# Gated linear attention into a gated state-space block: the second group's output product by seven half-block products, and where the weight sums lie

## The chip, the cores and the metric

The kernel runs on one core of a Trainium2 chip. The metric is the device time of one execution in microseconds, the median of several runs. Engine names follow the profile: PE (TensorE matmul), PEld (its weight loads), DVE (VectorE), ACT (ScalarE), POOL (GpSimd), SP (SyncE, which here only issues DMAs).

## The reference, cut to what matters

Batch 4, 8 heads, 768 steps, head size 48, model size 384, inner size 512, all in fp32:

```python
for t in range(S):                       # attention, per batch and head
    state = alpha[t][:, None] * state + outer(k[t], v[t])
    y[t] = q[t] @ state
x = y, heads side by side                # (4, 768, 384)
val, gate = split(x @ w_in)              # 2 x 512 columns
h[t] = exp(A_log) * h[t-1] + val[t]
f = silu(gate) * h
out = f @ w_out                          # (4, 768, 512) @ (512, 384)
```

The last line is what the change is about. `w_in` and `w_out` arrive as 64-bit floats and are turned to fp32 on the chip.

## The kernel before, in words

The 4 x 768 steps are cut into 12 groups of 256 steps (`n` = 0 to 11, three to a batch). A Python loop over `n` writes the whole order out by hand (`manual_schedule`), so each engine's queue is in program order, and an instruction waits only by semaphores for what it reads or overwrites. In the turn of group n, TensorE does the projections of group n (`project`, L988, four chunks `cc` of the inner size, 128 channels each), the attention of group m = n + 1 (`scores` L798, `values` L834, `states` L866, `carried` L847), and an output. DVE does, for a group two or so ahead, the transposes of alpha, k and q (L600), the running products P (`scan_P`, L635) and their inverses V (`scan_V`, L654), the scaled keys Zk (L619) and queries Zq (L610). For group n it does the state scan `hh` of each chunk (L995). The product f = silu(gate) x hh (L1008) is made on DVE for groups 0, 1 and 11 and on POOL for the others. Below, f0 to f3 and hh0 to hh3 are those of chunks 0 to 3.

The output f @ w_out of a group is done in one of two ways:

- `output` (L1011), groups 0 and 1: eight matmuls of 128x384 into two PSUM banks, two evictions on ACT (L1016), two DMAs from SP (L1017).
- `output_parts` (L1067), groups 2 to 10: the product is seen as a 2x2 by 2x2 block product and done with seven half-block products (L1064) in place of eight, each of two matmuls of 128x192. This needs sums of the weights, T1 to T4 (`sum_weights`, L1040 to L1044, on POOL, once), and sums of f, S1 to S4 (S3 at L1055 and S1 at L1058 on POOL, S2 and S4 at L1059 and L1060 on DVE). ACT copies three products out of PSUM (`s1`, `s7`, `s5`) and evicts a quarter; DVE adds the rest (U2 at L1092, then L1093 and L1094), POOL one quarter (L1090, L1095); SP sends the two rows blocks (L1097).

The seven products run on TensorE in the order written: pa with B11, pd with S3 and T3, then pc with S1 and T1, pa with B21 (it adds to the first one's bank), pd with T4, pb with S2 and T2, pc with S4 and B22. The profile counts every fp32 matmul twice, so a product of two matmuls stands as x4 and one whole output as x28.

`T1` to `T3` lie in `wide`, which in turn 0 and until the end of `output(0)` holds f of group 0. So `sum_weights` waits for that output's last matmul. f of groups 1 to 11 all lie in the one buffer `f_last`.

PSUM banks for projections, scores and outputs are four (`mm0` to `mm3`), and the string `taken` says by hand which one each request takes. A matmul into a bank waits until the bank's last reader is done. Three row buffers `o_sb` hold results on their way out.

In turn 1 (`n == 1`, L1229 to L1268) the part touched is, in order of writing: third(2) (its last DMAs are issued by POOL and SP at L963), f1, the scan V, project chunk 2, Zk, f2, `output(0)`, `sum_weights`, project chunk 3, transpose of q (L1264), its reload, Zq (L1266), f3, and the transposes of alpha and k for group 4; after it `output(1)` (L1348), and `first(3)`'s scores at the head of turn 2.

Of the kernel before, what the change touches and what calls it, by code (L numbers as in the profile page):

```python
# [9 lines left out]
FP32 = mybir.dt.float32  # L10
# [336 lines left out]
def fast(  # L347
# [22 lines left out]
    nc = tc.nc  # L370
    B, H, S, D = q.shape
    DM = H * D
    DI = moe_A_log.shape[0]
    C = 128
    G = 2
# [231 lines left out]
    def scaled_q(m, t, P, c=None):  # L607
        u0, n = (0, 2 * G) if c is None else (2 * c, 2)
        at = ds(u0 * L, n * L)
        nc.vector.tensor_mul(Zqs[m % 2][:, ds(u0, n), :, D:].rearrange("p u h t -> p h u t"),  # L610
                             t[:, :, at].rearrange("p h (u t) -> p h u t", t=L),
                             P[:, :, 1:GP][:, :, at].rearrange("p h (u t) -> p h u t", t=L))
# [48 lines left out]
    def products(m):  # L661
# [17 lines left out]

    taken = iter("0321032103231023" "1023102310231023" "102310231023" "10"
                 "23012301" "230132" "01230123" "012310" "23012301" "230132" "01230123" "012310"
                 "23012301" "230132" "01230123" "012310" "23012301" "230132" "01230123" "012310"
                 "23012301" "0132" "01320132")

    def bank(tag=None):
        if tag:
            return ps_at.tile([C, 512], FP32, tag=tag, name=tag)
        return ps_mm.tile([C, 512], FP32, tag=f"mm{next(taken)}", name="mm")  # L690
# [255 lines left out]
    for h in range(H):  # L946
        i, e, s = h // 4, h % 4 // 2, h % 2 ^ h // 4
        at = D * h
# [79 lines left out]
    HM = DM // 2  # L1028
    KC = NI // 2
    blocks = [[w_outs[k][:, :, ds(HM * i, HM)] for i in range(2)] for k in range(KC)]  # L1030
    flat = wide.rearrange("p c x -> p (c x)")
    sums_w = [flat[:, ds(KC * HM * i, KC * HM)].rearrange("p (a n) -> p a n", a=KC) for i in range(3)]
    T4 = [wide_S[i][:, 0:HM] for i in range(KC)]
    s1, s7 = flat[:, ds(3 * KC * HM, HM)], wide_S[2][:, 0:HM]
    parts_f = {}

    def sum_weights():
# [13 lines left out]
    def quarter(row, col):  # L1051
        return f_last[:, ds(KC * col, KC), ds(C * row, C)]
# [1 line left out]
    def sum_early():  # L1054
        nc.gpsimd.tensor_sub(parts_f["S3"], quarter(1, 0), quarter(0, 0))  # L1055

    def sum_late():
        nc.gpsimd.tensor_add(parts_f["S1"], quarter(1, 0), quarter(1, 1))  # L1058
        nc.vector.tensor_add(parts_f["S2"], quarter(1, 1), parts_f["S3"])  # L1059
        nc.vector.tensor_sub(parts_f["S4"], quarter(0, 1), parts_f["S2"])  # L1060

    def product(o, a, b, start):
        for k in range(KC):
            nc.tensor.matmul(o, a[:, k], b[k] if type(b) is list else b[:, k], start=start and k == 0,  # L1064
                             stop=k == KC - 1, skip_group_check=True)

    def output_parts(n):  # L1067
        b, g = divmod(n, NG)
        (B11, B12), (B21, B22) = blocks
        T1, T2, T3 = sums_w  # L1070
        S1, S2, S3, S4, U2, s5 = (parts_f[x] for x in ("S1", "S2", "S3", "S4", "U2", "s5"))
        copy = lambda to, t: nc.scalar.activation(to, t, AF.Copy)
        pa, pd = [bank()[:, 0:HM] for _ in range(2)]
        product(pa, quarter(0, 0), B11, True)
        copy(s1, pa)
        product(pd, S3, T3, True)
        yield
        copy(s7, pd)
        yield
        pc = bank()[:, 0:HM]  # L1080
        product(pc, S1, T1, True)
        copy(s5, pc)
        product(pa, quarter(0, 1), B21, False)
        o_sb = [rows.tile([C, DM], FP32, tag="o_sb", name="o_sb") for _ in range(G)]
        copy(o_sb[0][:, 0:HM], pa)
        product(pd, quarter(1, 1), T4, False)
        pb = bank()[:, 0:HM]
        product(pb, S2, T2, True)
        product(pc, S4, B22, False)
        nc.gpsimd.tensor_add(s7, s7, s5)  # L1090
        yield
        nc.vector.tensor_add(U2, s1, pb)  # L1092
        nc.vector.tensor_add(o_sb[1][:, 0:HM], U2, pd)  # L1093
        nc.vector.tensor_add(o_sb[0][:, HM:], U2, pc)  # L1094
        nc.gpsimd.tensor_add(o_sb[1][:, HM:], U2, s7)  # L1095
        for c in range(G):
            nc.sync.dma_start(out=out[b, ds(g * GC + c * C, C), :], in_=o_sb[c])  # L1097
        yield
# [16 lines left out]
    def go(count):  # L1115
        for _ in range(count):
            next(steps, None)
# [73 lines left out]
    for n in range(N):  # L1191
# [37 lines left out]
        elif n == 1:  # L1229
# [22 lines left out]
            load_raw("k", 4, nc.sync)  # L1252
            load_v(4, nc.sync)
            f1()
            junk(3)
            V = scan_V(3, P)
            f2 = project(n, 2)
            scaled_k(3, tk, V)
            f2()
            output(0)  # L1260
            sum_weights()
            f3 = project(n, 3)
            tq = plain("q")
            turn("q", tq)  # L1264
            load_raw("q", 4, nc.sync)
            scaled_q(3, tq, P)  # L1266
            f3()
            go(2)  # L1268
        else:
            if n == 2:  # L1270
                first(m)
# [72 lines left out]
            load_v(m + 2, nc.sync)  # L1344
        if n == N - 2:
            check_flag()
        if n == 1:
            output(n)  # L1348
        if n == N - 2:
            for _ in outs:  # L1350
                pass
# [5 lines left out]
@with_exitstack  # L1357
def kernel(ctx: ExitStack, tc: tile.TileContext, *args):
    nc = tc.nc
    out = args[-1]  # L1360
    C, GC, NI = 128, 256, 4
    B, S, DM = out.shape
    keep = ctx.enter_context(tc.tile_pool(name="keep", bufs=1))
    ps_mm = ctx.enter_context(tc.tile_pool(name="ps_mm", bufs=1, space=bass.MemoryType.PSUM))
    w_outs = [keep.tile([C, 2, DM], FP32, name=f"w_out{i}") for i in range(2)]
    f_last = keep.tile([C, NI, GC], FP32, name="f_last")
    rows = ctx.enter_context(tc.tile_pool(name="rows", bufs=3))
    with tc.manual_schedule():
        good = fast(tc, *args, w_outs, f_last, ps_mm, rows)
    with tc.If(good <= 0, preferred_fallthrough_block=True, label="last") as choice:  # L1370
        general(tc, *args, w_outs)
    with choice.Else(), tc.manual_schedule():
        half = DM // 2
        for i, c, at, size in ((0, 0, 0, DM), (1, 1, 0, half), (3, 1, half, half)):
# [41 lines left out]
```

## Time and profile before

| what | us |
|---|---|
| median of 3 runs (lowest, highest) | 269.58 (269.56, 270.09) |
| the profiled execution, its own time | 270.68 |
| its span in the trace | 269.0 |
| TensorE busy | 263.0 |
| VectorE busy | 233.5 |
| GpSimd busy | 165.3 |

The trace is of the profiled execution; the 1.68 us beside its span are start and end, which no engine shows. It ran 1.1 us longer than the median run. In the rows, a start is counted from the start of the span, and a duration is that of one instruction or, where "x" is above 1, of a merged run of them. The last part of a row in brackets is idle time ahead of it and who ended it.

### The profile page before, as it was taken

To read this page: it belongs to the slowest core of one execution; us is meant where nothing else is said; L and a number is where in the kernel's file an instruction comes from. 1 tells how busy PE (TensorE), PEld (TensorE's weight loads), DVE (VectorE), ACT (ScalarE), POOL (GpSimd) and SP (SyncE) were. 2 spreads that over 40 slices of the span, in tenths; PEclk is the share of its full clock that TensorE was granted. 3 is DMA by queue.
4 is the path that set the end of the run, shared out by engine and by line. 5 is a ranking of instruction groups with operands and counts; after the bars stand their busy time and mean duration, and the time that the engine had idled before them with its cause. 6 is when DMAs were issued, how large, how long until landed. Compare 5 with 4: busy or idle time off the path is not lost.

```text
span 269.0 us, 9976 instructions
## 1 busy us (share of the span) xinstructions
PE 263.0 (98%) x4168; PEld 230.2 (86%) x4168; DVE 233.5 (87%) x316; ACT 111.6 (41%) x270; POOL 165.3 (61%) x185
## 2 busy tenths in 40 slices
PE   7989999999999999999999999999999999999995
PEld 5978889886688988988988988988988989988974
DVE  7978898996999999999999999999999998883440
ACT  4666776281242631632543533524524515314011
POOL 8222304093267998996985995996886987646000
PEclk9999999999999999999999999999999999999999
DMA  5938974796993659559687478569588501201201
GB/s 173 316 117 281 296 172 139 210 225 159 243 220 90 138 159 231 119 140 229 133 227 170 107 207 184 113 173 219 128 210 172 144 3 29 75 3 37 70 7 59
DMA packets 52304, 41.19 MB, mean 153 GB/s; under 512 B 27392, under 2 KB 50944, under 8 KB 52256
## 3 DMA queue, kind: packets, MB, share of 16 engines
q1 hardware_dynamic: 49328, 37.34, 56.1%
q0 software_dynamic: 1536, 2.20, 3.1%
q10 hardware_dynamic: 1392, 0.99, 1.3%
q8 instruction: 34, 0.56, 0.9%
q14 instruction: 14, 0.11, 0.1%
HBM read 32.54 MB, written 4.72 MB: 139 GB/s over the span
## 4 chain that ended last, share of the span: by engine, by line
PE 96%; DMA 2%; issue 0%; ACTq 0%; ACT 0%
PE mm L988 48%; PE mm L1064 16%; PE y L834 4%; PE y L847 4%; PE mm L1022 4%; PE s L798 4%; PE mm L798 3%; PE s L866 3%; PE mm L707 2%; PE mm L1377 2%; DMA raw_q<-in_q_dram 2%; PE mm L702 2%; PE mm L703 1%; PE y L918 1%; PE mm L750 1%; PE y L926 1%
## 5 line engine op out<-in xcount | busy, mean ns | idle before, releaser
L988 PE MATMUL mm<-xT,w_in 128*128 128x256 f32 x576 | 129.4, 382 | 0.0
L988 PEld LDWEIGHTS mm<-xT,w_in 128*128 128x128 f32 x576 | 107.9, 190 | 16.0 <-issue 0.5
L1006 ACT ACTIVATE sg<-mm 128x256 f32<-128x256 f32 x48 | 18.4, 383 | 88.9 <-PE mm L988 88.9
L1008 POOL TENSOR_TENSOR f_last<-sg,hh 128x256 f32<-128x256 f32 x36 | 28.8, 806 | 26.1 <-ACT sg L1006 22.6
L886 POOL TENSOR_TENSOR sum<-sum,dS 128x192 f32<-128x192 f32 x30 | 39.3, 1310 | 3.0 <-ACT dS L874 1.4
L635 DVE TENSOR_TENSOR_SCAN P<-al,lower 128x1028 f32<-128x1028 f32 x12 | 30.5, 2541 | 0.3
L995 DVE TENSOR_TENSOR_SCAN hh<-a_dec,hh,mm 128x256 f32<-128x256 f32 x32 | 23.3, 728 | 8.4 <-PE mm L988 8.2
L654 DVE TENSOR_TENSOR_SCAN V<-al,ends 128x1028 f32<-128x1028 f32 x12 | 28.5, 2375 | 0.4
L963 POOL DMA_DIRECT2D xT<-yst x44 | 22.6, 518 | 5.4 <-ACT yst L960 4.0
L556 POOL TENSOR_TENSOR w_in<-w_in,wr 128x768 int32<-128x768 int32 x4 | 7.3, 1820 | 26.3 <-DVE wbits L1143 9.3
L1064 PE MATMUL mm<-wide,wr 128*128 128x192 f32 x108 | 20.8, 327 | 0.0
L600 DVE STREAM_TRANSPOSE k<-raw_k 128x1024 f32<-128x1024 f32 x9 | 18.5, 2053 | 0.0
L600 DVE STREAM_TRANSPOSE q<-raw_q 128x1024 f32<-128x1024 f32 x9 | 18.2, 2026 | 0.0
L1064 PEld LDWEIGHTS mm<-wide,wr 128*128 128x128 f32 x108 | 18.0, 190 | 0.0
L874 ACT ACTIVATE dS<-s 128x384 f32<-128x384 f32 (+1 forms) x18 | 7.4, 461 | 24.4 <-PE s L866 24.4
L818 POOL TENSOR_TENSOR AK<-AK,mask 128x512 f32<-128x512 f32 x9 | 13.7, 1520 | 5.9 <-ACT AK L814 5.7
L600 DVE STREAM_TRANSPOSE al<-raw_a 128x1024 f32<-128x1024 f32 x8 | 16.4, 2045 | 0.0
L619 DVE TENSOR_TENSOR Zk<-k,V 128x1024 f32<-128x1024 f32 (+1 forms) x14 | 15.8, 1128 | 0.1
L1064 PE MATMUL mm<-w_out,f_last 128*128 128x192 f32 x72 | 15.6, 339 | 0.0
L610 DVE TENSOR_TENSOR Zq<-q,P 128x1024 f32<-128x1024 f32 (+1 forms) x14 | 15.2, 1083 | 0.0
L847 PEld LDWEIGHTS y<-Zq,sum 48*64 48x64 f32 x656 | 11.6, 134 | 3.5 <-issue 3.0
L834 PE MATMUL y<-AK,v 64*64 64x64 f32 x352 | 14.5, 221 | 0.0
(188 smaller groups left out, 503.7 us busy)
## 6 DMA issues: line engine op xcount, KB each, us to landing
v<-in_v_dram SPq DMA_DIRECT2D x22, 192.0 KB, 3.6
out_dram<-o_sb SPq DMA_DIRECT2D x22, 192.0 KB, 2.7
raw_k<-in_k_dram SPq DMA_DIRECT2D x18, 184.0 KB, 4.6
raw_q<-in_q_dram SPq DMA_DIRECT2D x18, 184.0 KB, 4.7
raw_k<-in_k_dram SPq DMA_DIRECT2D x18, 176.0 KB, 4.9
raw_q<-in_q_dram SPq DMA_DIRECT2D x18, 176.0 KB, 4.7
wbits<-in_moe_w_in_dram SPq DMA_DIRECT2D x8, 384.0 KB, 5.7
raw_a<-in_alpha_dram SPq DMA_DIRECT2D x16, 184.0 KB, 3.6
```

The costliest lines, as they stand in the source:

```text
L600: nc.vector.transpose(out=by_runs(to).rearrange("p h c j -> p h j c"), in_=raws[name][:, 0:4 * ROW].rearrange("p (h j d) -> p h j d", h=4, ...
L635: nc.vector.tensor_tensor_scan(out=P, data0=al[:, 0:4 * GP], data1=lower.rearrange("p h t -> p (h t)"), initial=0.0, op0=ALU.mult, op1=ALU ...
L654: nc.vector.tensor_tensor_scan(out=V[:, ::-1], data0=al[:, 1:4 * GP + 1][:, ::-1], data1=ends.rearrange("p h t -> p (h t)")[:, ::-1], init ...
L798: nc.tensor.matmul(scs[m][c][i][ds(L * h, L), ds(p * (L + D), L + D)], Zk[rows, c, p, ds(h * L, L)], Zq[rows, u, p], start=True, stop=True ...
L834: nc.tensor.matmul(ys[m][i][ds(64 * s, 64), e, ds(c * C + h * L, L)], v_sb[rows, c, 4 * i + p, :], As[i][rows, c, p, :], start=across and ...
L847: nc.tensor.matmul(ys[m][i][ds(64 * s, 64), e, ds(u * L, L)], Ss[j][rows, p, :], Zqs[m % 2][rows, u, p, D:], start=False, stop=True, skip_ ...
L886: nc.gpsimd.tensor_add(Ss[j][:, :, 0:D], Ss[j - 1][:, :, 0:D], part)
L963: engines[n % len(engines)].dma_start(out=xT[to, a], in_=st[rows, i, e])
L988: nc.tensor.matmul((pv, pg)[vg], w_ins[cc][:, kk, vg, :], xT[:, kk, :], start=(kk == 0), stop=(kk == NK - 1))
L995: nc.vector.tensor_tensor_scan(out=hh, data0=a_dec[:, cc:cc + 1].to_broadcast([C, GC]), data1=pv, initial=prev_h[cc][:, GC - 1:GC] if n % ...
L1008: f = lambda: engine.tensor_mul(fs[n][cc], sg, hh)
L1064: nc.tensor.matmul(o, a[:, k], b[k] if type(b) is list else b[:, k], start=start and k == 0, stop=k == KC - 1, skip_group_check=True)
```

## The change

Group 1 is put through `output_parts` too, and `output(1)` goes away. T1 to T4 go into the low 32-bit words of the raw 64-bit bits of `w_out` (`wobits`): the conversion of `w_out` has read these, and the later check reads the high words alone. So T1 to T4 have a step of two words from element to element, `sum_weights` no longer waits for `output(0)`, and it is written ahead of the scan V of turn 1, together with S3 of group 1. `s1` moves to `wide_S[0]`. For group 1 alone, S2 and S4 are made on POOL, and the product of pa with B21 stands ahead of pc's. The transpose of q, its reload and Zq are written ahead of `output(0)`, which on DVE puts them ahead of hh3. The seven products stand behind f3, then the alpha transpose of group 4 (`go(1)`), the three DVE sums, and the k transpose (`go(1)`). The `taken` string and the three banks of the last group's output are renamed to go with it.

```diff
-    flat = wide.rearrange("p c x -> p (c x)")
-    sums_w = [flat[:, ds(KC * HM * i, KC * HM)].rearrange("p (a n) -> p a n", a=KC) for i in range(3)]
-    T4 = [wide_S[i][:, 0:HM] for i in range(KC)]
-    s1, s7 = flat[:, ds(3 * KC * HM, HM)], wide_S[2][:, 0:HM]
+    lows_out = [t.rearrange("p cc n two -> p (cc n) two")[:, :, 0].bitcast(FP32) for t in wobits]
+    sums_w = [t[:, ds(at, KC * HM)].rearrange("p (a n) -> p a n", a=KC)
+              for t, at in ((lows_out[0], 0), (lows_out[0], KC * HM), (lows_out[1], 0))]
+    T4 = [lows_out[1][:, ds((KC + i) * HM, HM)] for i in range(KC)]
+    s1, s7 = wide_S[0][:, 0:HM], wide_S[2][:, 0:HM]
...
-    def sum_late():
+    def sum_late(engine=nc.vector):
         nc.gpsimd.tensor_add(parts_f["S1"], quarter(1, 0), quarter(1, 1))
-        nc.vector.tensor_add(parts_f["S2"], quarter(1, 1), parts_f["S3"])
-        nc.vector.tensor_sub(parts_f["S4"], quarter(0, 1), parts_f["S2"])
+        engine.tensor_add(parts_f["S2"], quarter(1, 1), parts_f["S3"])
+        engine.tensor_sub(parts_f["S4"], quarter(0, 1), parts_f["S2"])
...
+        def first_quarter():
+            product(pa, quarter(0, 1), B21, False)
+            copy(o_sb[0][:, 0:HM], pa)
+
+        if n == 1:
+            first_quarter()
         pc = bank()[:, 0:HM]
         product(pc, S1, T1, True)
         copy(s5, pc)
-        product(pa, quarter(0, 1), B21, False)
-        copy(o_sb[0][:, 0:HM], pa)
+        if n > 1:
+            first_quarter()
...
             f1()
+            sum_weights()
+            sum_early()
             junk(3)
             V = scan_V(3, P)
             f2 = project(n, 2)
             scaled_k(3, tk, V)
             f2()
-            output(0)
-            sum_weights()
-            f3 = project(n, 3)
             tq = plain("q")
             turn("q", tq)
             load_raw("q", 4, nc.sync)
             scaled_q(3, tq, P)
+            output(0)
+            f3 = project(n, 3)
             f3()
-            go(2)
+            sum_late(nc.gpsimd)
+            outs = output_parts(n)
+            for _ in range(3):
+                next(outs)
+            go(1)
+            next(outs)
+            go(1)
...
-        if n == 1:
-            output(n)
```

TensorE's order does not change but for the output itself: project chunk 2, `output(0)`, project chunk 3, the output of group 1, scores of group 3.

More of the change, by code (lines that the diff above doesn't have):

```diff
@@ L678, in products @@
         yield
[L682 to L685, printed above, removed]
+    taken = iter("0321032103231023" "1023102310231023" "1023102310" "2301" "23"
+                 "10321032" "103201" "32103210" "321023" "10321032" "103201" "32103210" "321023"
+                 "10321032" "103201" "32103210" "321023" "10321032" "103201" "32103210" "321023"
+                 "10321032" "3201" "32013201")
     def bank(tag=None):
@@ L1079, in output_parts @@
         yield
+        o_sb = [rows.tile([C, DM], FP32, tag="o_sb", name="o_sb") for _ in range(G)]
+        def first_quarter():
[3 more added lines that the diff above has]
+            first_quarter()
         pc = bank()[:, 0:HM]
@@ L1082, in output_parts @@
         copy(s5, pc)
-        product(pa, quarter(0, 1), B21, False)
-        o_sb = [rows.tile([C, DM], FP32, tag="o_sb", name="o_sb") for _ in range(G)]
-        copy(o_sb[0][:, 0:HM], pa)
+        if n > 1:
+            first_quarter()
         product(pd, quarter(1, 1), T4, False)
@@ L1373 @@
         half = DM // 2
-        for i, c, at, size in ((0, 0, 0, DM), (1, 1, 0, half), (3, 1, half, half)):
+        for i, c, at, size in ((3, 0, 0, DM), (2, 1, 0, half), (0, 1, half, half)):
             o = ps_mm.tile([C, 512], FP32, tag=f"mm{i}", name="mm")[:, 0:size]
```

## The prediction

> **What bounds the kernel now.** I read the page's totals and its chain first, then the chain in order of time around the change, then DVE and POOL there.
>
> ```profile
> span 269.0 us, 9976 instructions
> PE 263.0 (98%) x4168; PEld 230.2 (86%) x4168; DVE 233.5 (87%) x316; ACT 111.6 (41%) x270; POOL 165.3 (61%) x185
> PE 96%; DMA 2%; issue 0%; ACTq 0%; ACT 0%
> ```
>
> TensorE is busy for 98% of the span and 96% of the chain is its own work. So a microsecond off TensorE's queue is one off the end, as long as nothing makes TensorE wait. DVE at 87% is the engine to watch.
>
> ```profile
> 59.56 5.16 PE mm L1022 x16
> 64.72 2.59 PE mm L988 x12
> 67.31 5.16 PE mm L1022 x16
> 72.47 0.93 PE s L798 x32
> ...
> 87.59 0.77 PE s L798 x32
> 88.36 0.77 PE mm L798 x32
> 89.13 4.75 PE mm L1064 x28
> ...
> 95.22 10.56 PE mm L988 x48
> ```
>
> The chain in order of time (start, length, line): `output(0)` at 59.56, project chunk 3, `output(1)` at 67.31, scores of group 3 at 72.47. The same output by seven products, for group 2, takes 4.75 at 89.13. There is no gap between the pieces.
>
> ```profile
> 59.03 2.30 DVE L654 TENSOR_TENSOR_SCAN V<-al,ends 128x1028 f32<-128x1028 f32 x1
> 62.03 1.20 DVE L619 TENSOR_TENSOR Zk<-k,V 128x1024 f32<-128x1024 f32 x1
> 63.15 0.41 DVE L1008 TENSOR_TENSOR f_last<-sg,hh 128x256 f32<-128x256 f32 x1
> 66.06 0.75 DVE L995 TENSOR_TENSOR_SCAN hh<-a_dec,hh,mm 128x256 f32<-128x256 f32 x1 [2.50 <-PE mm L988]
> 66.72 2.03 DVE L600 STREAM_TRANSPOSE q<-raw_q 128x1024 f32<-128x1024 f32 x1
> 68.78 1.43 DVE L610 TENSOR_TENSOR Zq<-q,P 128x1024 f32<-128x1024 f32 x1
> 70.14 0.41 DVE L1008 TENSOR_TENSOR f_last<-sg,hh 128x256 f32<-128x256 f32 x1
> 70.47 2.02 DVE L600 STREAM_TRANSPOSE al<-raw_a 128x1024 f32<-128x1024 f32 x1
> 72.34 2.04 DVE L600 STREAM_TRANSPOSE k<-raw_k 128x1024 f32<-128x1024 f32 x1
> ...
> 124.25 0.75 DVE L995 TENSOR_TENSOR_SCAN hh<-a_dec,hh,mm 128x256 f32<-128x256 f32 x1 [0.44 <-PE mm L988]
> ```
>
> ```profile
> 58.32 2.02 POOL L963 DMA_DIRECT2D xT<-yst  x4
> 64.88 0.99 POOL L1040 TENSOR_TENSOR wide<-w_out,w_out 128x384 f32<-128x384 f32 x1 [4.54 <-PE mm L1022]
> 65.83 0.99 POOL L1041 TENSOR_TENSOR wide<-w_out 128x384 f32<-128x384 f32 x1
> 67.99 1.14 POOL L1044 TENSOR_TENSOR wide_S<-w_out,wide 128x192 f32<-128x192 f32 x2
> ```
>
> DVE and POOL in order of time. DVE has one hole, 2.50 us ahead of hh3; the next row with idle time ahead of it is the last one here, at 124.25. POOL makes T1 to T4 in about 4.2 us, beside DVE work that is mostly a transpose.
>
> **The change part by part.** The output: 5.16 goes, 4.75 comes, **-0.41** on the chain. That is the whole direct gain, 0.15% of 269; the rest is whether the operands are there in time.
>
> When they are due: a product is 4.75 / 7 = 0.68. From 67.31 the seven start at 67.31 (pa), 67.99 (pd, needs S3), 68.67 (pa again, needs f2 and f3), 69.35 (pc, S1), 70.03 (pd, T4), 70.7 (pb, S2), 71.4 (pc, S4). Before, the last two chunks' matmuls stood at the end of the two banks, and f3 ended at 70.55 without harm. Now f3 is due 1.9 sooner. If DVE ran unhindered it would be: q, Zq, hh3 and f3 fill the hole from 63.5, taking by their distance to the next start 1.87 (the alpha transpose's), 1.11 (row below), 0.66 and 0.33, so f3 ends at 67.5, over 1 us early.
>
> But the sums now stand elsewhere. POOL comes free at 58.32 + 2.02 = 60.34, in the middle of the scan V, and then runs T3, T1, T2, T4, S3 beside DVE's Zk, f2 and Zq. What such neighbours do to each other:
>
> ```profile
> 74.90 2.27 DVE L635 TENSOR_TENSOR_SCAN P<-al,lower 128x1028 f32<-128x1028 f32 x1
> 92.41 3.29 DVE L635 TENSOR_TENSOR_SCAN P<-al,lower 128x1028 f32<-128x1028 f32 x1
> 85.34 1.17 DVE L610 TENSOR_TENSOR Zq<-q,P 128x1024 f32<-128x1024 f32 x1
> ```
>
> ```profile
> 74.88 3.36 POOL L818 TENSOR_TENSOR AK<-AK,mask 128x512 f32<-128x512 f32 x1 [5.75 <-ACT AK L814]
> 83.58 0.73 POOL L1055 TENSOR_TENSOR wr<-f_last 128x256 f32<-128x256 f32 x1
> 91.69 1.29 POOL L818 TENSOR_TENSOR AK<-AK,mask 128x512 f32<-128x512 f32 x1
> 92.93 0.60 POOL L886 TENSOR_TENSOR sum<-sum,dS 128x192 f32<-128x192 f32 x1
> ```
>
> A POOL AK that takes 1.29 alone takes 3.36 beside a scan P of 2.27: it waits for all of it. The other way about, the scan at 92.41 takes 3.29, 1.02 more than 2.27, and its 2.27 fit only from 93.43: it waited for AK (to 92.98) and also for the L886 queued behind it (to 93.53). The q transpose at 66.72, with one operand, ran 2.03 beside T1 and T2, and these took their 0.99: no collision.
>
> So, step by step, the likeliest way: T3 waits for V (to 61.33) and ends at 62.2. Zk arrives at 62.03, but T1 stands right behind T3 and needs nothing of it; as L886 did, it goes first, to 63.15. Zk (1.12 to the next start) to 64.27. T2, which waits for T1 and then for Zk, to 65.2. f2 to 65.55. q's transpose to 67.4; beside it T4's pair (1.14) and S3 (0.73), done at 67.45. Zq 1.11 to 68.5, hh3 to 69.2, **f3 to 69.55**. On TensorE pd is in time; pa waits until 69.6, and five products of 0.68 stand behind it: end at 73.0. S1, S2, S4 on POOL at 0.73 each end at 70.3, 71.05, 71.8, against pc at 70.3, pb at 71.6, pc at 72.3: just in time. Scores of group 3 start at 73.0 in place of 72.47: **+0.5**, the gain gone and as much again lost.
>
> The other order would be: where only first come counts. The Trainium skill, SBUF — State Buffer, section "Who interferes with whom", says that a DVE instruction with two SBUF inputs contends with a GpSimd one that reads SBUF, and that whoever issues first gets the shared ports for the whole instruction. The blocking agrees with 3.36 against 1.29; the order doesn't with the scan at 92.41, which had come before L886. By that rule the sum would be the first rival's below.
>
> Behind it, DVE: the three sums (L1092 to L1094, 0.35 each) wait for pb and for pc's last product, so the k transpose starts at 73.0 + 0.5 = 73.5 in place of 72.34: DVE is 1.15 late, TensorE 0.5. AK of group 3 (tied to scores) then comes at 75.4, ahead of the scan P, which waits for it to 76.7: DVE 1.75 late. Zq of group 4 ended at 86.51 and scores of group 4 started at 87.59, a margin of 1.08; now 88.26 against 88.09: **+0.2**.
>
> ```profile
> 95.97 0.35 DVE L1093 TENSOR_TENSOR o_sb<-wr,mm 128x192 f32<-128x192 f32 x1
> ```
>
> The next tight place: L1093 frees the bank that chunk 0's gate matmuls of group 3 want at 95.22 + 1.32 (six of 48 passes of 0.22) = 96.54; it ends at 96.32, margin 0.22. DVE's 1.75 would break it, but the scan at 92.41 now arrives at 94.16, about when AK and L886 are through (93.53 + 0.7), and gets its 1.02 back: 97.07 against 97.24. I take 0; if the scan collides again it is up to +0.55. Behind it DVE catches up, as the idle time at 124.25 shows, so I count nothing more.
>
> The queues: q's reload on SP now stands ahead of `output(0)`'s DMAs.
>
> ```profile
> 68.78 1.78 SPq L411 DMA_DIRECT2D raw_q<-in_q_dram  x4
> out_dram<-o_sb SPq DMA_DIRECT2D x2, 192.0 KB, 3.3
> ```
>
> Reload from 67.4 to 69.2, then the first row block, 3.3 us to landing: about 72.8. L1093 of group 1 writes that row buffer at about 72.7, so it may wait 0.1 (0 to 0.5, on DVE alone, and its bank is wanted by scores only at 73.8). I take 0, inside the range. ACT trades two evictions for four shorter copies with idle time around them: 0. Alpha's and k's reloads for group 5 go out 2 us later and are read a whole turn later: 0.
>
> The step of two words: TensorE reads T1 to T4, four of seven products in ten groups, at twice the spacing. No matmul in this trace reads a spaced operand. From below: no gain, the columns stay 192. From above: a spaced 192 could cost as much as the 384 words it spans, 5.16 / 16 - 4.75 / 28 = 0.153 a pass, 16 passes, 10 groups, +24 us. The nearest row is a DVE conversion that reads every second word of `wobits`:
>
> ```profile
> 53.69 0.55 DVE L549 TENSOR_SCALAR w_out<-wobits 128x768 uint32<-128x768 uint32 x1
> L556 POOL TENSOR_TENSOR w_in<-w_in,wr 128x768 int32<-128x768 int32 x4 | 7.3, 1820 | 26.3 <-DVE wbits L1143 9.3
> ```
>
> 0.55 for 768 is no slower per element than the rows without a step (0.75 for 256), so I take 0. For POOL's T1 to T4 likewise 0; from above the 1.82 of a 128x768, 0.83 more each, which delays S3 and the end by up to 2.5. The Trainium skill, Advanced Engine Details and Errata, section "Memory Cachelines", asks for two hits on a 16-byte line for full speed, which a step of two words has; no run here shows it.
>
> **The rivals.**
> 1. First come, first served (25%). Zk to 63.3, T1 to 64.25, f2 to 64.6, q to 66.45, Zq from 66.6 to 67.7, hh3 and f3 to 68.75; S3, behind Zq, at 68.45. Six products from 68.45: 72.5, +0.05, and the margin at scores of group 4 gives +0.2: 269.8. For it, S1 on POOL and S4 on DVE of another group, where they take turns behind S2:
>
> ```profile
> 126.88 0.97 POOL L1058 TENSOR_TENSOR wr<-f_last 128x256 f32<-128x256 f32 x1
> 127.30 0.84 DVE L1060 TENSOR_TENSOR wr<-f_last,wr 128x256 f32<-128x256 f32 x1
> ```
>
> 2. On the other side: no collision that matters (17%). f3 by 68.6 and S3 by 67.9 decide: then no product waits, -0.41, with 0 to 0.2 lost again at scores of group 4: 269.2 to 269.4. Against it: T3 can hardly start ahead of V's end.
> 3. The spacing costs TensorE or POOL (5%): by the bounds above 272 to 294.
>
> **How the numbers follow.** The forecast, +0.5 +0.2 = +0.7, has 53%: profiled 270.68 + 0.7 = 271.4; on the median, which lies 1.1 under the profiled run, 269.58 + 0.7 = **270.3**, its own range +0.55 to +1.4, 270.1 to 271.0. From 269.0 (rival 2 with the spread of the runs) to 271.2 (both open collisions and the row buffer) more than 8 in 10 lie. A measurement of this kernel can tell about 0.2%, 0.54 us, from no change. Slower: forecast 50% (3% of it stay within) and rival 3, 55%. Faster: 4% of rival 2. Same: the rest, 41%.
>
> **What would show it.** T3 ending with V and T1 ahead of Zk; f3 ending near 69.5; x28 of L1065 from 67.3 taking 5.5 to 5.7 with a wait ahead of the third product; scores of group 3 near 73.0; a short wait for Zq at scores of group 4; passes of the later outputs still 4.75 in all. Wrong would be: f3 by 68.6 (rival 2), 4.75 gone up in every group (rival 3), or a wait for a row buffer above 0.5.

## The result, and the profile after

The changed kernel is slower: 273.13 us (median of 7 runs, 272.61 to 275.72) against 270.09 beside it (269.40 to 271.56), a ratio of 1.0122 (95% interval 1.0097 to 1.0147). Run a second time it came to 272.40 against 270.12, 1.0084 (1.0063 to 1.0105). The forecast was 270.3 with a range to 271.2: the sign of the likeliest case was right, its size was not, and the time lies outside the range. Of the 2.83 us between 273.13 and 270.3, 0.51 is the base: the kernel before, counted on with 269.58, took 270.09 here. Of several kernels below single executions come out 1.5% and more longer than their fastest; the ratios leave those out.

The page of the changed kernel: the span, the engines' busy time, and the chain's shares.

```profile
span 274.0 us, 10018 instructions
PE 265.1 (97%) x4180; PEld 233.5 (85%) x4180; DVE 240.2 (88%) x319; ACT 112.2 (41%) x272; POOL 168.8 (62%) x191
PE 79%; DVE 10%; POOL 3%; ACT 2%; issue 2%; DMA 1%; SPq 1%; DVEq 0%; POOLq 0%; ACTq 0%
```

The last line matters most: before, 96% of the chain was TensorE's own work, now it is 79%, and 10% of the chain runs over DVE and 3% over POOL. Where, the waits of TensorE tell. A row gives the line that waits and who ended the wait, then the total in us, how often, and the longest:

```profile
PE mm L1065 <- DVE f_last L1008: 1.8, 1, 1.8
PE mm L988 <- DVE hh L995: 1.6, 1, 1.6
PE y L847 <- POOL sum L886: 0.5, 1, 0.5
PE mm L1065 <- POOL wr L1059: 0.2, 1, 0.2
```

Before, there was no wait of TensorE in these turns. This execution took 275.72, the longest of its seven, and one wait in it, for hh2's bank (L988), isn't in the second run of the same kernel, whose profiled execution took 272.34. The second run is the base of the comparisons below:

```profile
PE mm L1065 <- DVE f_last L1008: 0.9, 1, 0.9
PE y L847 <- POOL sum L886: 0.6, 1, 0.6
PE mm L1065 <- POOL wr L1059: 0.2, 1, 0.2
```

What sets the two apart starts in rows that the change doesn't touch, the conversion of `w_out` in turn 1. DVE and POOL of the longest execution, then of the second run:

```profile
53.56 2.25 DVE L551 TENSOR_SCALAR wr<-wobits 128x768 uint16<-128x768 uint16 x1
...
59.84 1.19 DVE L1008 TENSOR_TENSOR f_last<-sg,hh 128x256 f32<-128x256 f32 x1
...
61.16 2.89 DVE L654 TENSOR_TENSOR_SCAN V<-al,ends 128x1028 f32<-128x1028 f32 x1
...
53.52 1.82 POOL L556 TENSOR_TENSOR w_out<-w_out,wr 128x768 int32<-128x768 int32 x1 [6.95 <-ACT wr L543]
...
59.74 1.01 POOL L1041 TENSOR_TENSOR wobits<-w_out,w_out 128x384 f32<-128x384 f32 x1
```

```profile
52.88 0.64 DVE L551 TENSOR_SCALAR wr<-wobits 128x768 uint16<-128x768 uint16 x1
...
57.78 2.30 DVE L654 TENSOR_TENSOR_SCAN V<-al,ends 128x1028 f32<-128x1028 f32 x1
```

A conversion of 0.64 took 2.25: it ended 0.47 behind the POOL sum beside it (53.52 + 1.82 = 55.34). DVE was so late that T3 (L1041, at 59.74) came ahead of f1 (59.84) and V, and every later step moved. In the second run the same POOL sum came at 52.83, 0.05 ahead of the conversion, which still took its 0.64: the start of a row doesn't tell who goes first of two that come so close.

To compare stages, the following table counts the first row of each stage on TensorE in the timeline from the first matmul of `output(0)`, since what lies before differs by up to 1.3 us between the profiled executions.

| profiled execution of | output of group 1 | scores of group 3 | scores of group 4 | output of group 2 | last matmul's end |
|---|---|---|---|---|---|
| before | 7.75 | 13.00 | 28.01 | 29.66 | 206.22 |
| after, second run | 7.75 | 14.12 | 29.92 | 31.57 | 209.16 |

The loss has three places: 1.12 up to the scores of group 3, 0.79 more up to those of group 4, and 206.22 - 29.66 = 176.56 grown to 177.59, 1.03, over the rest.

**What I take to be the causes, and the rivals.** (1) T1 to T4 with a step of two words cost TensorE a little in every output. (2) In turn 1 the weight sums on POOL stand beside V, Zk, f2 and Zq and make f3 and S1 late. (3) In turn 2 DVE is late because its three sums wait for the last products and take DVE's time, and the lateness is paid at POOL's state sums or at Zq. The rivals: the time is lost in the queues, the banks or the row buffers; or the early sums cost by themselves, whatever reads them.

### The profile page after: what moved, and what is told of

Its sections match the earlier page's. It is cut to its first block, busy times and chain, and to the rows that moved or that the text cites. A ratio compares the mean times of both kernels' runs of the same rounds, so it can differ in the third digit from the quotient of the medians.

```text
span 274.0 us, 10018 instructions
## 1 busy us (share of the span) xinstructions
PE 265.1 (97%) x4180; PEld 233.5 (85%) x4180; DVE 240.2 (88%) x319; ACT 112.2 (41%) x272; POOL 168.8 (62%) x191
## 4 chain that ended last, share of the span: by engine, by line
PE 79%; DVE 10%; POOL 3%; ACT 2%; issue 2%; DMA 1%; SPq 1%; DVEq 0%; POOLq 0%; ACTq 0%
PE mm L988 40%; PE mm L1065 17%; PE y L834 4%; PE y L847 4%; PE mm L798 3%; PE s L798 3%; DVE P L635 3%; PE s L866 3%; PE mm L1390 2%; DVE V L654 2%; PE mm L707 1%; DMA raw_k<-in_k_dram 1%; PE y L779 1%; POOL sum L886 1%; DVE q L600 1%
## 5 line engine op out<-in xcount | busy, mean ns | idle before, releaser
L988 PE MATMUL mm<-xT,w_in 128*128 128x256 f32 x576 | 129.3, 382 | 1.7 <-DVE hh L995 1.6
L988 PEld LDWEIGHTS mm<-xT,w_in 128*128 128x128 f32 x576 | 107.9, 190 | 17.7 <-DVE hh L995 2.2
L1008 POOL TENSOR_TENSOR f_last<-sg,hh 128x256 f32<-128x256 f32 x36 | 28.0, 784 | 30.6 <-ACT sg L1006 24.1
L886 POOL TENSOR_TENSOR sum<-sum,dS 128x192 f32<-128x192 f32 x30 | 39.5, 1318 | 3.3 <-ACT dS L874 1.8
L654 DVE TENSOR_TENSOR_SCAN V<-al,ends 128x1028 f32<-128x1028 f32 x12 | 29.2, 2437 | 0.4
L1065 PE MATMUL mm<-wobits,wr 128*128 128x192 f32 x120 | 24.2, 333 | 0.2 <-POOL wr L1059 0.2
L556 POOL TENSOR_TENSOR w_in<-w_in,wr 128x768 int32<-128x768 int32 x4 | 7.3, 1823 | 25.9 <-DVE wr L551 16.1
L1065 PEld LDWEIGHTS mm<-wobits,wr 128*128 128x128 f32 x120 | 20.6, 188 | 0.5 <-POOL wr L1059 0.5
L1065 PE MATMUL mm<-w_out,f_last 128*128 128x192 f32 x80 | 17.5, 338 | 1.8 <-DVE f_last L1008 1.8
L1065 PEld LDWEIGHTS mm<-w_out,f_last 128*128 128x128 f32 x80 | 13.0, 188 | 3.4 <-DVE f_last L1008 2.0
L847 PE MATMUL y<-Zq,sum 48*64 48x64 f32 x656 | 14.3, 222 | 0.5 <-POOL sum L886 0.5
```

The source lines that it names most:

```text
L654: nc.vector.tensor_tensor_scan(out=V[:, ::-1], data0=al[:, 1:4 * GP + 1][:, ::-1], data1=ends.rearrange("p h t -> p (h t)")[:, ::-1], init ...
L847: nc.tensor.matmul(ys[m][i][ds(64 * s, 64), e, ds(u * L, L)], Ss[j][rows, p, :], Zqs[m % 2][rows, u, p, D:], start=False, stop=True, skip_ ...
L886: nc.gpsimd.tensor_add(Ss[j][:, :, 0:D], Ss[j - 1][:, :, 0:D], part)
L988: nc.tensor.matmul((pv, pg)[vg], w_ins[cc][:, kk, vg, :], xT[:, kk, :], start=(kk == 0), stop=(kk == NK - 1))
L1008: f = lambda: engine.tensor_mul(fs[n][cc], sg, hh)
```

## The experiments

### The changed kernel again

> The changed kernel once more, for a second trace of it. Theory 1 (the sums T1 to T4 on POOL stand ahead of f1 and of the scan V on the two engines' shared access, so hh2 and f3 come late): the same two waits of TensorE, about 1.6 us ahead of project chunk 3 and about 2 us ahead of the second pa product, wherever the early part of the run lands. Rival 1 (the trace after was unlucky: the w_out conversion on DVE at 53.6 lost 1.6 us to a POOL addition, which the change does not touch): in a run where that conversion is not held, as in the trace before, the waits shrink to under 1 us together and the span to about 271.

272.40 (272.32 to 272.71), with the waits and the stages shown above. Rival 1 of the expectation came out for the wait ahead of project chunk 3, which is gone, and nearly for the rest: the two waits of the output add up to 1.1, and the span is 270.6.

### Before, with T1 to T4 alone in the low words

```diff
-    sums_w = [flat[:, ds(KC * HM * i, KC * HM)].rearrange("p (a n) -> p a n", a=KC) for i in range(3)]
-    T4 = [wide_S[i][:, 0:HM] for i in range(KC)]
+    lows_out = [t.rearrange("p cc n two -> p (cc n) two")[:, :, 0].bitcast(FP32) for t in wobits]
+    sums_w = [t[:, ds(at, KC * HM)].rearrange("p (a n) -> p a n", a=KC)
+              for t, at in ((lows_out[0], 0), (lows_out[0], KC * HM), (lows_out[1], 0))]
+    T4 = [lows_out[1][:, ds((KC + i) * HM, HM)] for i in range(KC)]
```

> The kernel before, with T1 to T4 kept in the low words of w_out's bits and nothing else moved: group 1 by eight products, the sums after the first output. If the spacing costs TensorE what the later outputs show (4.86 against 4.75 each), nine outputs give +1.0 us, time 0.3 to 0.4% over before and outputs of 4.86. If the spacing costs nothing and the 4.86 come from another placing of waits, no difference within 0.1%.

272.08 (270.74 to 274.15), 1.0075 (1.0048 to 1.0101). Its chain of waits at the scores and the output in turn 2:

```profile
86.74 0.77 PE s L798 x32
87.51 0.77 PE mm L798 x32
88.28 4.86 PE mm L1065 x28
```

No product waits, the stages of turns 1 and 2 are those of before (13.00, 28.01), and the same seven products take 4.86 in place of 4.75: 0.11 an output. The nine outputs of groups 2 to 10 make 9 x 0.11 = 1.0, and the last matmul ends 1.03 later (207.25). So the spacing costs TensorE by itself. The time is 1.96 over before, more than this 1.03. Part of the rest is no work of an engine: in the median 1.95 lie outside the span in this kernel and 1.72 in the kernel before, and in the profiled execution 3.1 (272.28 against a span of 269.2). The spans themselves are 1.3 longer in the median (269.7 against 268.4). Why more lies outside the span isn't known.

### The changed kernel with T1 to T4 side by side

```diff
-        hi = bits_of(i)[0][:, :, :, 1].bitcast(FP32)
+        hi = bits_of(i % NI)[0][:, :, :, 1].bitcast(FP32)
...
-    lows_out = [t.rearrange("p cc n two -> p (cc n) two")[:, :, 0].bitcast(FP32) for t in wobits]
-    sums_w = [t[:, ds(at, KC * HM)].rearrange("p (a n) -> p a n", a=KC)
-              for t, at in ((lows_out[0], 0), (lows_out[0], KC * HM), (lows_out[1], 0))]
-    T4 = [lows_out[1][:, ds((KC + i) * HM, HM)] for i in range(KC)]
+    words = wobits[0].rearrange("p cc n two -> p (cc n two)").bitcast(FP32)
+    sums_w = [words[:, ds(KC * HM * i, KC * HM)].rearrange("p (a n) -> p a n", a=KC) for i in range(3)]
+    T4 = [words[:, ds((3 * KC + i) * HM, HM)] for i in range(KC)]
```

> The changed kernel with T1 to T4 side by side over all words of one half of w_out's bits, so without the step of two words; the range check of w_out is replaced by one more of w_in of the same size, since its words are overwritten. If the spacing is 0.11 a group: outputs of 4.75, 1.1 us under the changed kernel, about 0.7% over before. If spacing also slows POOL's sums, these get shorter than 1.0 us each and the waits of turn 1 shrink as well. If spacing costs nothing: the same time as the changed kernel.

271.72 (271.44 to 272.02), 1.0053 (1.0036 to 1.0071). The page's group of the products that read T1 to T3 (busy time, mean ns of one), first of the changed kernel's second run, then of this one:

```profile
L1065 PE MATMUL mm<-wobits,wr 128*128 128x192 f32 x120 | 24.1, 333 | 0.2 <-POOL wr L1059 0.2
```

```profile
L1064 PE MATMUL mm<-wobits,wr 128*128 128x192 f32 x120 | 23.3, 328 | 0.2 <-POOL wr L1058 0.2
```

0.8 us less busy time for 120 passes, 7 ns a pass; over the 16 passes of an output that read T1 to T4 this is the 0.11. The stages of turns 1 and 2 stay late (14.02, 29.82), and 208.03 - 31.46 = 176.57 is the rest of before. So the spacing makes the 1.03 and nothing of turns 1 and 2.

### The changed kernel without the weight sums

```diff
...
-    T4 = [lows_out[1][:, ds((KC + i) * HM, HM)] for i in range(KC)]
+    sums_w = [blocks[0][1], blocks[1][1], blocks[0][1]]
+    T4 = [blocks[1][0][:, i] for i in range(KC)]
...
-        nc.gpsimd.tensor_sub(T3, B12, B22)
-        nc.gpsimd.tensor_sub(T1, B12, B11)
-        nc.gpsimd.tensor_sub(T2, B22, T1)
-        for i in range(KC):
-            nc.gpsimd.tensor_sub(T4[i], B21[:, i], T2[:, i])
```

> The changed kernel with the sums T1 to T4 left out; the products read blocks of w_out in their place, without a step. Theory 1: f1, V, Zk and f2 are not held, hh2 is done by 62, f3 by 68.6, no wait of TensorE above 0.3 us in turn 1, time at or below before, -0.4 to 0 us. Rival 2 (the seven products themselves stall on f3 and on S1, S2, S4, which q's transpose and Zq push behind, whatever POOL does with T): a wait of about 2 us ahead of the second pa product stays, and the time is 1.5 us or more over before.

This kernel leaves out T1 to T4, so its output is not the reference's. 271.22 (270.56 to 272.13), 1.0030 (1.0014 to 1.0046), not the time at or below before that was expected. Scores of group 3 stand at 12.70, 0.30 ahead of before: with the sums gone the late f3 is gone. But scores of group 4 stand at 29.16: turn 2 takes 16.46 in place of 15.01. TensorE's waits here:

```profile
PE y L847 <- POOL sum L886: 0.6, 1, 0.6
PE mm L798 <- DVE o_sb L1092: 0.3, 1, 0.3
```

Its timeline, DVE and then SP's queue, shows who ended the wait of DVE's second sum:

```profile
71.86 0.35 DVE L1092 TENSOR_TENSOR o_sb<-wr,mm 128x192 f32<-128x192 f32 x1 [1.12 <-DMA out_dram<-o_sb]
```

```profile
64.74 3.28 SPq L411 DMA_DIRECT2D raw_q<-in_q_dram  x4
68.11 0.85 SPq L1017 DMA_DIRECT2D out_dram<-o_sb  x2
```

DVE waits for a row buffer, because q's reload (3.28 of SP's queue) was put ahead of `output(0)`'s DMAs. So the weight sums explain turn 1, and turn 2 is lost without them too. How much of that is DVE's three sums alone this run doesn't show, since the wait for the row buffer delays DVE by another 1.12; the kernels below, where the reload stands behind those DMAs, separate the two.

### The changed kernel with Zq of group 3 behind hh3 and f3

```diff
-            scaled_q(3, tq, P)
             output(0)
             f3 = project(n, 3)
             f3()
+            scaled_q(3, tq, P)
```

> The changed kernel with Zq of group 3 on DVE behind hh3 and f3 of group 1 in place of ahead of them. If the wait ahead of the second pa product (0.9 to 1.1 us, by DVE's f3) comes from f3 being late by T's sums plus Zq, f3 ends 1.2 us sooner, that wait goes, and scores of group 3 start 13.1 us after the first output in place of 14.1; the later wait for POOL's state sums in turn 2 and the spacing stay, so about 1 us under the changed kernel. If S1 (POOL, behind f3) or the T sums hold the products instead, the wait moves to the pc product and little is won.

272.86 (272.07 to 277.08), 1.0100 (1.0064 to 1.0136): no faster, as in the second case of the expectation. f3 comes 1.4 sooner (S1, which starts behind it, at 67.41 - 58.35 = 9.06 in place of 68.57 - 58.12 = 10.45) and the wait for it goes, but POOL's S1, free at the same moment as Zq, is held by it:

```profile
67.41 1.65 POOL L1059 TENSOR_TENSOR wr<-f_last 128x256 f32<-128x256 f32 x1 [1.39 <-DVE f_last L1008]
```

1.65 in place of 0.73, and TensorE waits 0.9 for S1. Scores of group 3 stand at 13.64, 0.48 sooner than with Zq in front; those of group 4 at 29.44.

### The changed kernel with S3 of group 2 behind the state sums

```diff
-            if n < N - 1:
+            if n < N - 1 and n != 2:
                 sum_early()
             if n - 1 in late:
                 second(m)
+                sum_early()
```

> The changed kernel with S3 of group 2 (0.73 on POOL) behind the state sums of group 3 in place of ahead of them, in turn 2. If TensorE's wait in turn 2 (0.6 to 1.0 us ahead of the carried matmuls, by POOL's state sum) is there because DVE, late behind the three new sums, runs Zq of group 4 into the second state sum, the sums end 0.7 us sooner and ahead of Zq, the wait goes, and the time is 0.8 us under the changed kernel. If it is Zq itself that TensorE lacks, nothing changes.

273.40 (272.88 to 276.55), 1.0145 (1.0099 to 1.0190). The wait for POOL's state sum is gone and another has come:

```profile
PE s L798 <- DVE Zq L610: 0.4, 1, 0.4
```

Turn 2, from scores to scores, takes 15.55 in place of 15.80, before 15.01. Both end at the same lateness of DVE: with the POOL sum out of the way, Zq itself is what TensorE waits for. The 0.25 is given back later (the last matmul ends at 209.14, before the move at 209.16). That the time is 1.0 above that of the second run isn't the move: in this profiled execution `output(0)` began 0.87 later.

### Unspaced sums, with Zq, q's reload and S3 moved

T1 to T4 lie in pieces of 192 words that were free (one half of T4 keeps the step), Zq stands behind f3, q's reload behind `output(0)`'s DMAs, S3 of group 2 behind the state sums, as above.

```diff
...
+    t1 = const.tile([C, KC * HM], FP32, name="t1")
+    sums_w = [[t1[:, ds(HM * i, HM)] for i in range(KC)],
+              [wide[:, i, ds(2 * GC, HM)] for i in range(KC)],
+              [wide_S[i][:, 0:HM] for i in range(KC)]]
+    T4 = [wide_S[2][:, 0:HM], lows_out[1][:, 0:HM]]
...
-            load_raw("q", 4, nc.sync)
-            scaled_q(3, tq, P)
             output(0)
+            load_raw("q", 4, nc.sync)
             f3 = project(n, 3)
             f3()
+            scaled_q(3, tq, P)
             sum_late(nc.gpsimd)
...
```

> Seven products for group 1 with what the traces point to: 15 of 16 half blocks of T without spacing (in wide's unused columns, wide_S and a new small tile), Zq behind f3, q's reload behind the first output's DMAs, S3 of group 2 behind the state sums. If these four causes are all of the loss, only the 0.41 of the eighth product is left, less what DVE's three sums still cost: outputs of 4.75, scores of group 3 at 12.6 to 12.8 after the first output, 269.5 to 270.0, at or just under the kernel before. If the early sums on POOL cost by themselves whatever stands around them, it stays 0.3% or more over.

271.35 (271.00 to 276.25), 1.0043 (1.0026 to 1.0060), above the 269.5 to 270.0 expected. S1 is held by Zq here too (TensorE waits 0.7), scores of group 3 stand at 13.37, and turn 2 takes 15.56, with a wait of 0.4 for Zq. These two places make 0.92 of the 1.35 by which the last matmul ends later than before (207.57). Whether the early sums cost by themselves, the expectation's other case, is what the next run tests.

### Before, with the sums in the low words and early

As the second experiment, and `sum_weights` written ahead of the scan V; group 1 keeps its eight matmuls.

```diff
+            sum_weights()
             junk(3)
             V = scan_V(3, P)
...
             output(0)
-            sum_weights()
```

> The kernel before with T1 to T4 in the low words and formed early, ahead of f1 and V, but group 1's output by eight products as before. If the early sums hurt by delaying hh2 and f3 as such, TensorE waits ahead of project chunk 3 or in the second output and scores of group 3 come later than 13.0 after the first output. If they hurt only because seven products want f3 1.9 us sooner, TensorE has no new wait, and only the spacing is left, +1.0 us, as in the run with the spacing alone.

271.51 (271.00 to 273.57), 1.0054 (1.0033 to 1.0074). The sums run at the changed kernel's place and hold DVE as there, and the stages are 13.01 and 28.01, those of before. The last matmul ends at 207.55, 0.30 behind the run with the spacing alone; this 0.30 arises behind turn 2, and its cause is open. So the early sums cost nothing in turns 1 and 2 as long as nothing reads f3 early; with seven products in group 1 they do.

### Unspaced sums, with Zq behind the alpha transpose too; and DVE without group 1's sums

The first of the two moves one line of the kernel with unspaced sums above:

```diff
-            scaled_q(3, tq, P)
             sum_late(nc.gpsimd)
             outs = output_parts(n)
             for _ in range(3):
                 next(outs)
             go(1)
+            scaled_q(3, tq, P)
             next(outs)
```

> Like the kernel with unspaced sums (all of w_out's sums in pieces of 192 words side by side, Zq of group 3 behind f3, q's reload behind the DMAs of output(0), S3 of group 2 behind the state sums), but with Zq of group 3 behind the alpha transpose too, so that POOL's S1 isn't held by it. Theory A (every place that DVE loses at group 1's three sums is given back in turn 2): no product waits any more, scores of group 3 12.5 to 12.9 after output(0)'s first matmul (13.37 with Zq right behind f3, 13.00 before), but turn 2 still takes 15.4 to 15.8 in place of 15.0, so scores of group 4 stand at 28.1 to 28.6 (before 28.01), and the time is 270.2 to 270.9 against 270.1 before. Rival B (the operands' dates in turn 1 are all that counts): turn 2 takes 15.0, scores of group 4 at 27.5 to 27.7, and the time is 0.4 under before, 269.6 to 269.8.

270.12 (270.01 to 271.29) against 269.99, 1.0008 (0.9992 to 1.0023). Scores of group 3 come at 12.47, 0.53 ahead of before. Those of group 4 come at 28.03, 0.02 behind before: all of it is given back in turn 2, at the wait for Zq (turn 2 takes 15.56, as theory A has it). The last matmul ends at 206.67, 0.45 behind before: group 2's output, too, takes 5.02 in place of 4.76. The second kernel takes DVE's three sums away; ScalarE copies the three banks instead, so that the output of group 1 is not the reference's:

```diff
+        if n == 1:
+            copy(U2, pb)
+            copy(o_sb[1][:, 0:HM], pd)
+            copy(o_sb[0][:, HM:], pc)
+        else:
             nc.vector.tensor_add(U2, s1, pb)
...
```

> Like best2, but for group 1 alone the three sums of products on DVE are left out: ScalarE copies the three banks instead, so that DVE doesn't wait for the last products (that output is then not the reference's; the number of matmuls, evictions, DMAs and banks is the same). Theory A: turn 2 goes back to 15.0 to 15.2, scores of group 4 at 27.5 to 27.9, time 269.5 to 270.0, about 0.5 under best2. Rival B: no different from best2 within 0.2. A third case: ScalarE frees the banks or the row buffer later than DVE did, and TensorE waits 0.3 to 0.6 for a bank at the scores of group 3.

269.76 (269.08 to 274.30) against 269.99, 0.9975 (0.9954 to 0.9996). Turn 2 takes 15.01, TensorE waits for nothing from `output(0)` on, scores of group 4 stand at 27.48, 0.53 ahead of before, and the last matmul ends at 205.81, 0.41 ahead. The two timelines show the turning point, DVE's scan P and POOL's AK of group 3; first with DVE's sums, then without:

```profile
73.52 0.40 DVE L813 TENSOR_TENSOR A<-mm,mask 128x256 f32<-128x256 f32 x1
73.85 2.81 DVE L635 TENSOR_TENSOR_SCAN P<-al,lower 128x1028 f32<-128x1028 f32 x1
...
73.22 1.28 POOL L818 TENSOR_TENSOR AK<-AK,mask 128x512 f32<-128x512 f32 x1 [1.65 <-ACT AK L814]
```

```profile
72.68 0.39 DVE L813 TENSOR_TENSOR A<-mm,mask 128x256 f32<-128x256 f32 x1
73.01 2.27 DVE L635 TENSOR_TENSOR_SCAN P<-al,lower 128x1028 f32<-128x1028 f32 x1
...
73.27 3.09 POOL L818 TENSOR_TENSOR AK<-AK,mask 128x512 f32<-128x512 f32 x1 [1.63 <-ACT AK L814]
```

With the sums, AK comes 0.63 ahead of P and P waits for it (2.81); without them P comes 0.26 ahead of AK, runs its 2.27, and AK, which nothing needs soon, waits (3.09). Counted from `output(0)` (58.27 and 58.32), DVE is 0.89 later at P's start and 1.43 at its end. The first is the three sums themselves, three rows of 0.35 that keep DVE from 70.38 to 71.29 without a wait; the other 0.54 is P's wait for AK.

### Group 1's sums on POOL

The last kernel, made whole again: POOL adds what ScalarE copied.

```diff
...
             copy(o_sb[0][:, HM:], pc)
+            nc.gpsimd.tensor_add(U2, s1, U2)
+            nc.gpsimd.tensor_add(o_sb[1][:, 0:HM], U2, o_sb[1][:, 0:HM])
+            nc.gpsimd.tensor_add(o_sb[0][:, HM:], U2, o_sb[0][:, HM:])
```

> Like best2, but for group 1 alone ScalarE copies the three banks of the products to SBUF and POOL then adds them up (three more sums of 128x192, about 0.6 each), so that DVE has none of them and doesn't wait for the last products. The output is whole. Theory A (DVE's wait and work at these sums was what gave the gain back): POOL's sums fit between its last product sum (ends about 71) and AK of group 3 (due about 73.3 behind the scan P), so the stages stand as in the kernel with the sums left out: scores of group 3 12.5 after output(0)'s first matmul, turn 2 15.0 to 15.2, scores of group 4 27.5 to 27.7, time 269.3 to 269.9 against 270.0 before. Rival: POOL's sums hold Zq or the masks of group 3 on DVE, or AK comes ahead of the scan P, and turn 2 takes 15.4 or more: no faster than best2.

The trace has what was expected: 12.47, 15.00, scores of group 4 at 27.47, the last matmul's end at 205.81, no wait of TensorE from `output(0)` on. Its chain is TensorE's own work alone here:

```profile
66.50 4.63 PE mm L1071 x28
71.13 0.93 PE s L798 x32
...
86.24 0.77 PE s L798 x32
87.01 0.77 PE mm L798 x32
87.78 4.76 PE mm L1071 x28
```

The time doesn't follow it wholly: 270.30 (269.01 to 276.06) against 270.13, above the 269.3 to 269.9 expected, and a ratio of 0.9991 (0.9965 to 1.0017), no difference that can be told. The profiled execution took 269.46; what longer executions of this kernel wait for is in no trace. So no version here is shown to beat the kernel before.

## Why the prediction was wrong, by its own steps

Three terms of the sum were too small: the step of two words, put at 0, cost 1.03; f3's lateness, put at +0.5, cost 1.12 with what followed from it; turn 2, put at +0.2, cost 0.79, and at another operand than the one named.

- **The direct gain, -0.41: right in sign, a little small.** With every operand in time (the last two kernels) group 1's output takes 4.63, not the 4.75 of the other groups, and the scores behind it come 0.53 sooner. The last matmul ends 206.22 - 205.81 = 0.41 sooner; the 0.12 between are 176.69 against 176.56 over the rest, where one half of T4 still has the step (two passes in nine outputs, 18 x 0.007 = 0.13).
- **The step of two words, taken as 0: wrong**, and the largest single miss. It costs 0.11 an output, 1.03 over groups 2 to 10, 7 ns on a pass of 192 columns (about 4% of 4.75 / 28 = 0.170). I went by a DVE conversion that reads such words at no cost. That row is another engine's; for TensorE no row of the profile bore on it, only the bounds 0 to +24, and the third rival had this case right in kind: its bounds of 272 to 294 hold the time measured, but by the sum of three losses, as the spacing alone makes only 1.03. A step of two words is what the Trainium skill, Advanced Engine Details and Errata, section "Memory Cachelines", would have free, with two hits on a 16-byte line; here the measurement differs and decides. For POOL the 0 was right: T1 took 0.99 before (65.83) and 0.99 after (60.84, below).
- **f3 late, +0.5: right that the sums on POOL make it late, the size was half, and one link was right by luck.** The second run of the changed kernel on DVE and POOL, in order of time:

```profile
60.00 0.90 DVE L642 TENSOR_SCALAR ratio<-P 128x4 f32<-128x4 f32 x1
...
60.89 0.73 DVE L995 TENSOR_TENSOR_SCAN hh<-a_dec,hh,mm 128x256 f32<-128x256 f32 x1
61.55 1.38 DVE L619 TENSOR_TENSOR Zk<-k,V 128x1024 f32<-128x1024 f32 x1
62.84 1.23 DVE L1008 TENSOR_TENSOR f_last<-sg,hh 128x256 f32<-128x256 f32 x1
63.99 2.05 DVE L600 STREAM_TRANSPOSE q<-raw_q 128x1024 f32<-128x1024 f32 x1
66.08 1.22 DVE L610 TENSOR_TENSOR Zq<-q,P 128x1024 f32<-128x1024 f32 x1
67.22 0.74 DVE L995 TENSOR_TENSOR_SCAN hh<-a_dec,hh,mm 128x256 f32<-128x256 f32 x1
68.07 0.43 DVE L1008 TENSOR_TENSOR f_last<-sg,hh 128x256 f32<-128x256 f32 x1
```

```profile
59.09 1.79 POOL L1041 TENSOR_TENSOR wobits<-w_out,w_out 128x384 f32<-128x384 f32 x1
60.84 0.99 POOL L1042 TENSOR_TENSOR wobits<-w_out 128x384 f32<-128x384 f32 x1
61.91 1.87 POOL L1043 TENSOR_TENSOR wobits<-w_out,wobits 128x384 f32<-128x384 f32 x1
...
68.57 0.73 POOL L1059 TENSOR_TENSOR wr<-f_last 128x256 f32<-128x256 f32 x1 [2.78 <-DVE f_last L1008]
```

  T3 waits for V and ends 0.80 behind it, T1 goes ahead of Zk, T2 is queued between Zk and f2: the order of the forecast, not of the first rival. But T1 doesn't come first for the reason forecast. A small DVE step behind V (L642, 0.14 before at 61.24) is held to T3's end and takes 0.90, so hh2 and Zk come later, and when Zk starts at 61.55 T1 has been running since 60.84. That a POOL sum queued behind a running one passes a DVE instruction that is already waiting, as at 92.41, is therefore not tested here; the forecast didn't have L642's delay.

  Counted from `output(0)` (58.12 here, 59.40 before), T3 ends at 2.76 (forecast 2.8), Zk at 4.81 (4.87), q's transpose at 7.92 (8.0), f3 at 10.38 (10.15). On this scale the forecast's 73.0 for the scores of group 3 is 13.60, +0.60, and the 1.12 are this 0.60, 0.23 for f3, and 0.29 from f3's end to the scores (68.50 to 72.24, 3.74 in place of 3.45). In that stretch POOL begins S1 when f3 ends and takes 0.73; pc, which reads it, starts 0.86 behind f3 (69.36), where the forecast had 0.75 ("just in time"), and TensorE waits 0.2. From pc's start the four products take 2.88 in place of 2.7: the first, behind the wait, 0.78 where an unhindered one takes 0.68, and three of the four read spaced words.
- **Turn 2, +0.2 for Zq: the wrong place.** DVE's lateness was forecast well: AK comes ahead of P, P takes 2.88, and Zq ends 2.02 later than before, 0.90 more than TensorE's 1.12. That is inside Zq's margin of 1.08, and TensorE doesn't wait for Zq; it waits for POOL's second state sum (L886), held by Zq. Before, and in the second run after:

```profile
84.68 2.31 POOL L886 TENSOR_TENSOR sum<-sum,dS 128x192 f32<-128x192 f32 x2
...
86.94 0.65 PE L847 MATMUL y<-Zq,sum 48*64 48x64 f32 x32
```

```profile
86.06 1.19 DVE L610 TENSOR_TENSOR Zq<-q,P 128x1024 f32<-128x1024 f32 x1
...
85.41 2.29 POOL L886 TENSOR_TENSOR sum<-sum,dS 128x192 f32<-128x192 f32 x2
```

  It was held by Zq before as well, and ended at 86.99 - 59.40 = 27.59. The products that read it are the second 16 of the 32 from 86.94 on (in the second run TensorE waits behind the first 16), so the margin was hardly 0.1 (an estimate from these rows and the next), where I had read 1.08 off Zq. After, the sum ends at 87.70 - 58.12 = 29.58, 1.99 later, with TensorE 1.12 late: of the 0.87 between, 0.79 is TensorE's loss and the rest that margin.
- **The row buffer, taken as 0 (0 to 0.5): mostly right.** In the second run the three sums follow each other without it. It came, at 1.12, in the kernel without weight sums, where TensorE is sooner, and at 0.4 and 0.2 in the kernels with Zq behind f3 and with T1 to T4 side by side.
- **"Behind it DVE catches up": right.** In the kernel with T1 to T4 side by side the rest of the execution is that of before (176.57, 176.56).
- **The margin of the result.** The terms are +1.12, +0.79 and +1.03 against +0.5, +0.2 and 0. They add to 2.94 by the stages, and the time grew by 2.3 to 3.0. The second run's `output(0)` began 1.28 sooner than in the profiled execution of before, which the change doesn't explain: 0.84 of it is one idle stretch of TensorE in the trace of before, ahead of 20.16 (L926), that no instruction is seen to end and that the second run hasn't; the rest I can't assign.

That the weight sums and DVE's sums are the causes of turns 1 and 2 is shown by leaving them out, and that the spacing is the cause of the rest by the spacing alone and by the sums side by side. Of the rivals, the early sums cost nothing in turns 1 and 2 with eight products in group 1; the renamed banks are in the last two kernels too, where TensorE waits for none; the row buffer, behind q's reload on SP's queue, isn't waited for in the changed kernel's second run, whose losses these are. What else the longest execution of the changed kernel lost, beyond the conversion held in turn 1 and what moved with it, is not shown.

## What to carry to other kernels

Before an operand is moved to where it has a step, time one product that reads it so: a few per cent of a pass in the bottleneck, over all groups, outweigh a gain in one group. A margin is read at every operand that the stalled matmuls read, not only at the one whose producer moved: here Zq had 1.08 and the POOL sum held behind it hardly 0.1. And when work that waits for the last product is put on an engine that is 87% busy and feeds the next stage, the gain can be paid back there: in the traces here it was, until that work went to engines with idle time.

## What was not expected of the hardware

- A fp32 matmul with 192 moving columns a step of two words apart took 333 ns in the mean against 328, and an output of 28 passes, 16 of them so spaced, 0.11 more (4.86 against 4.75).
- Small DVE instructions are held by a POOL neighbour as large ones are: f2 took 1.23 beside T2 (0.41 before), L642 with its four columns 0.90 beside T3 (0.14), a conversion 2.25 beside L556 (0.64). The other way about, S1 on POOL took 1.65 beside Zq (0.73).
- Which of two goes first can turn on less than the start times show: in the longest execution DVE's conversion at 53.56 was held by POOL's sum of 53.52, and in the trace of before DVE's at 54.16 took 0.61 beside POOL's of 54.12, the same 0.04 ahead.
- The scan P of the next turn waited in the second run as in the trace of before: it came at 93.14, and its 2.27 fit only from 93.74, behind a POOL L886 that began after it, at 93.25.
